# The first super-step of a delta-rule attention and two MoE layers on one core, issued in a new order

## The chip, the core and the metric

The kernel runs on one core of a Trainium2 chip. The core has TensorE (PE: matmuls; its weight loads, PEld, overlap them), VectorE (DVE), ScalarE (ACT), GpSimd (POOL) and SyncE (SP), which issues most of the DMAs. Each engine works through its own queue in order and waits at an instruction until its inputs are there. The metric is the time of one execution on the device in microseconds (us), lower is better.

## The reference

A gated delta rule over 768 positions for 4 x 8 heads of 48 dimensions, and two MoE layers without routing on the 3072 tokens that come out of it:

```python
for t in range(S):
    kt, vt, bt = (k_n[:, :, t], v[:, :, t], beta[:, :, t, None])
    y[:, :, t] = np.einsum('bhd,bhde->bhe', q[:, :, t], state)
    v_old = np.einsum('bhde,bhd->bhe', state, kt)
    state = state + bt[:, :, :, None] * np.einsum('bhd,bhe->bhde', kt, vt - v_old)
...
h = np.maximum(x @ w_in, 0.0); x = h * h @ w_out          # 384 -> 2048 -> 384
g = x @ w_gate; out = g * sigmoid(g) * (x @ w_val) @ w_out2   # 384 -> 1536 -> 384
```

q, k, v and beta are float32; the MoE weights are float64 and reach the chip as pairs of 32-bit words.

## The kernel before

**Super-steps.** The sequence is cut into six super-steps J of 128 positions, each of two chunks c of 64 positions, each with two groups p of heads. For one chunk the recurrence is solved as a block: the gram matrix of k, times -1, a triangular mask and beta, gives M; the inverse of (1 - M) is needed (in NT0 for chunk 0, NT1 for chunk 1); then `ks` (V minus K times state), `u` (inverse times V), `y` (output) and `ku` (new state). Small matmuls in float32 do this on TensorE, with evictions by ScalarE and VectorE.

**The inverse.** For super-step 0 the 16x16 diagonal blocks are inverted on VectorE (`invert16`, once for each chunk). M goes out to DRAM and comes back with one small matrix per partition (`d_out`, `d_in`, tile T), and the result goes home again (`d_home`). Then `dt`, `d1`, `d2` (tiles `ps_dt`, `ps_d`, `ps_e`) merge 16 to 32, and `t11`, `m1`, `m2` (`ps_tq`, `ps_m`, `ps_x`) merge 32 to 64. For later super-steps 32x32 blocks are inverted on GpSimd (`invert`, 60 products and sums, lines 455 and 462), a super-step ahead: `gram`, `mout`, `tload`, `inv`, `nout`, `nback`.

**MoE 1.** For each super-step 16 blocks m of 128 hidden units: `moe1_h` makes `ps_h` (line 784: nine matmuls from x and weight, each split in a high part and a low part: xh, xl, wh, wl), ScalarE and VectorE make `hh` and `hl`, and `moe1_o` adds to `ps_y` (line 810). In super-step 0 the first `HMS[0]` = 14 blocks are done for the first half of the tokens (chunk 0, 256 columns), then again for the second half (chunk 1), so that work can begin before chunk 1 is there; the rest, and the later super-steps but for their first block, run 512 columns wide. MoE 2 comes after all of MoE 1.

**Weights.** 16 pieces (two blocks of `w_in`, or of `w_out`, 768 KB each, the last one in two) are converted from float64: ScalarE takes the absolute value of the upper word (line 173, tile f), VectorE does four integer steps (lines 180, 182, 186, 191, on f and raw), ScalarE writes the high part (line 204), and VectorE or GpSimd subtracts it for the low part (line 207, tile w). `conv(n)` does n of these quarter steps, `need` makes sure of a piece before its use, and during super-step 0 `slot` converts ahead at a rate of CR.

**What sets the order.** TensorE and SP run in the order in which the program is written. In the start (up to `PRE`) VectorE and GpSimd do too, and ScalarE is placed by the scheduler. In the loop that follows only VectorE (and TensorE, SP) keep program order; `timed` spreads the attention's steps over the MoE blocks. V of a chunk is multiplied by the norm (`vn`, line 307); for chunk 1 of super-step 0 this is written behind the inversion of super-step 1, on the same engine. `bank` and the tiles M and ys (two buffers together) limit how far evictions run ahead.

Of the kernel before, what the change touches and what calls it, by code (L numbers as in the profile page):

```python
# [8 lines left out]
F32 = mybir.dt.float32  # L9
# [11 lines left out]
def delta_attention_moe_moe2_kernel(  # L21
# [35 lines left out]
    nc = tc.nc  # L57
# [10 lines left out]
    HMS = [14, 1, 1, 1, 1, 1]  # L68
# [320 lines left out]
    def d_home(c):
        nc.sync.dma_start(  # L390
            out=d_scr[c].rearrange("a g x s t -> (a g x) (s t)"), in_=TF[c * 64:c * 64 + 64, 0:1024]
        )
        for a in range(2):
            for g in range(2):
                p0 = g * 64 + a * 32
                nc.sync.dma_start(
                    out=NT2[c][p0:p0 + 32, :, a * 32:(a + 1) * 32], in_=d_scr[c, a, g].rearrange("x s t -> s x t")
                )
# [68 lines left out]
    def invert16(c):  # L467

        pr = slice(64 * c, 64 * c + 64)
        t_ = TF[pr].rearrange("p (a k) -> p a k", a=2)[:, :, 0:512].rearrange("p a (i j) -> p a i j", j=32)  # L470
        for kk in range(14, 0, -1):
            w = 15 - kk
            tmp = TMP[pr, 0:2 * kk * w].rearrange("p (a i j) -> p a i j", a=2, j=w)
            nc.vector.tensor_tensor(
                tmp,
                t_[:, :, 0:kk, kk:kk + 1].to_broadcast([64, 2, kk, w]),
                t_[:, :, kk:kk + 1, kk + 1:16].to_broadcast([64, 2, kk, w]),
                op=ALU.mult,
            )
            rows = t_[:, :, 0:kk, kk + 1:16]  # L480
            nc.vector.tensor_tensor(rows, rows, tmp, op=ALU.add)
        nc.vector.memset(TF[pr, 0:1024:33], 1.0)

# [195 lines left out]
    def do_y(J, c, p):  # L679
# [3 lines left out]
    STAGES = {  # L683
        "loadk": (k_load, 0), "norm": (k_norm, 0), "nout": (n_out, 0), "gram": (gram, 0.9),
# [5 lines left out]
        "sq": (k_squares, 0), "root": (k_root, 0), "gram0": (gram0, 0.9), "m0": (m0, 0), "dout": (d_out, 0),  # L690
        "din": (d_in, 0), "inv0": (invert16, 0), "dhome": (d_home, 0),
# [236 lines left out]
    order.enter_context(tc.manual_schedule(engines={mybir.EngineType.DVE, mybir.EngineType.Pool}))  # L928

    def conv(n, lo=nc.vector):  # L930
        conv_to(converted() + n, lo)
# [3 lines left out]
    def stage(w, J, c):  # L935
        run_all((w, J, c, p) for p in P2)

    make_identity(nc, ident)
# [6 lines left out]
    nc.gpsimd.memset(AQT[32:64, :, 1], 0.0)  # L945
    for p in P2:
        nc.gpsimd.memset(RSF[p], 0.0)
    nc.sync.dma_start(out=bB, in_=beta)
    run(("loadk", 0, 0))
    run(("loadk", 0, 1))  # L950
    load_w1(0, 0)

    nc.vector.reduce_sum(lower, ident.rearrange("p (b z k) -> p z b k", z=2, k=16)[:, 1], axis=AX.XY)
# [19 lines left out]
    load_w1(1, 0)
    run(("dhome", 1))
    run(("loadk", 1, 1))
    load_w1(1, 1)
    conv(4)
    for w in ("dt", "d1", "d2"):
        run_all((w, 0, p) for p in P2)
    run(("norm", 1, 0))  # L980
    stage("t11", 0, 0)
    stage("m1", 0, 0)
    run(("norm", 1, 1))
    load_w1(2, 0)
    run_all([("gram", 1, 0, 0, True), ("mout", 1, 0, 0)])
    stage("m2", 0, 0)
    run_all([("gram", 1, 1, 0, True), ("mout", 1, 1, 0)])
    conv(3)
    stage("u", 0, 0)
    load_w1(2, 1)  # L990
    stage("y", 0, 0)
    run(("fetch", 0, 0, TOK // 2))
    conv(4)
    run_all([("gram", 1, 0, 1, True), ("mout", 1, 0, 1)])
    stage("ku", 0, 0)
# [3 lines left out]
    for w in ("dt", "d1", "d2"):  # L999
# [8 lines left out]
    conv(4)  # L1008
    PRE = converted()
    startup.clear()  # L1010

# [10 lines left out]
    if True:  # L1022

        LOW2 = 300
        LEAD = 1
        MID = 11
# [3 lines left out]
        CR = 0.75  # L1030
# [17 lines left out]
        timed = spread([L], LEAD, mid) + spread(plan(1, 2, PG, GA, AA, NA, TA), mid, 2 * NM1 + HMS[1] - END)  # L1048
# [127 lines left out]
```

## Time and profile before

| | |
|---|---|
| median of 3 runs | 1242.2 us (1238.1 to 1243.32) |
| profiled execution | 1241.77 us, its span 1239.9 us |
| PE busy | 1099.2 us (89%) |
| PEld, DVE, ACT, POOL busy | 919.8, 626.0, 397.9, 277.9 us |
| mean granted PE clock | 0.944 |

Busy time is the union of an engine's instructions. A timeline row gives start, duration, engine, line, operation, output <- inputs, shapes, count, and in brackets the idle time before it with the instruction that ended that. The granted clock is 1.00 at 2.4 GHz and 0.50 at 1.2 GHz; a mean between them is a mixture.

### The profile page before, as it was taken

What the parts mean: (1) busy time and instruction counts of PE and PEld (TensorE: products, weight loads), DVE (VectorE), ACT (ScalarE), POOL (GpSimd) and SP (SyncE); (2) the same over time, 40 slices, a digit from 0 to 9 for tenths busy, and PEclk for the clock granted to TensorE, in tenths of its full rate; (3) what the DMA queues carried; (4) which work ended last, traced back from release to release, by engine and by line L of the source; (5) the groups of instructions that cost most, each with busy time, mean ns of one, the idle gap of its engine ahead of it and who ended that gap; (6) DMA issues with size and microseconds to landing.
All of it is one profiled execution on the core that took longest, in us unless ns stands there. A gap on an engine that the chain in (4) does not pass through costs nothing. (4 is left out here: it accounts for less than half of the span.)

```text
span 1239.9 us, 25325 instructions
## 1 busy us (share of the span) xinstructions
PE 1099.2 (89%) x10971; PEld 919.8 (74%) x10971; DVE 626.0 (50%) x1034; ACT 397.9 (32%) x753; POOL 277.9 (22%) x396
## 2 busy tenths in 40 slices
PE   3454566799999999999999998799999999999998
PEld 3444555689788888878888876578888888888887
DVE  5751452653664755665545379963434333343333
ACT  1333333334423323332333466631212222121221
POOL 2038321028207405713700023410000000000000
PEclk9977576599999999999999999999999999999999
DMA  7656003443432622613321144510101000010000
GB/s 169 180 116 244 1 7 69 87 108 68 122 80 45 153 66 49 166 44 69 72 56 27 51 154 152 182 48 1 51 1 52 1 31 21 1 51 1 26 1 26
DMA packets 129696, 88.24 MB, mean 71 GB/s; under 512 B 103217, under 2 KB 107953, under 8 KB 129585
## 3 DMA queue, kind: packets, MB, share of 16 engines
q1 hardware_dynamic: 128384, 81.64, 25.4%
q0 software_dynamic: 1056, 4.72, 1.0%
q8 instruction: 86, 1.41, 0.5%
q10 hardware_dynamic: 144, 0.26, 0.1%
q14 instruction: 26, 0.20, 0.1%
HBM read 63.54 MB, written 23.07 MB: 70 GB/s over the span
## 5 line engine op out<-in xcount | busy, mean ns | idle before, releaser
L784 PE MATMUL ps_h<-xh,w 128*128 128x512 f32 (+1 forms) x720 | 222.4, 372 | 46.9 <-DVE w L207 29.0
L784 PEld LDWEIGHTS ps_h<-xh,w 128*128 128x128 f32 x720 | 137.5, 203 | 68.6 <-DVE w L207 29.2
L810 PE MATMUL ps_y<-hh,w 128*128 128x512 f32 (+1 forms) x690 | 165.1, 377 | 10.4 <-ACT w L204 8.7
L877 PE MATMUL ps_g<-x2h,w 128*128 128x512 f32 x432 | 145.7, 392 | 0.5 <-ACT x2h L862 0.5
L787 ACT ACTIVATE r<-ps_h 128x512 f32<-128x512 f32 (+1 forms) x120 | 61.3, 511 | 263.6 <-PE ps_h L784 248.4
L877 PE MATMUL ps_v<-x2h,w 128*128 128x512 f32 x432 | 144.7, 389 | 0.0
L810 PEld LDWEIGHTS ps_y<-hh,w 128*128 128x128 f32 x690 | 119.9, 200 | 30.9 <-ACT w L204 9.1
L881 DVE SCALAR_TENSOR_TENSOR th<-th,ps_g 128x512 f32<-128x512 f32 x72 | 49.5, 687 | 167.6 <-ACT th L880 167.4
L784 PE MATMUL ps_h<-xl,w 128*128 128x512 f32 (+1 forms) x360 | 130.5, 363 | 1.5 <-DVE xl L666 1.5
L794 DVE TENSOR_TENSOR hl<-r,hh 128x512 fp32r<-128x512 f32 (+1 forms) x120 | 79.7, 665 | 88.5 <-ACT r L792 78.8
L790 DVE TENSOR_TENSOR r<-r 128x512 f32<-128x512 f32 (+1 forms) x72 | 49.1, 682 | 135.5 <-ACT hh L788 135.2
L902 PE MATMUL ps_o<-ph,w 128*128 128x512 f32 x432 | 111.9, 389 | 2.7 <-ACT ye L826 2.7
L810 PE MATMUL ps_y<-hl,w 128*128 128x512 f32 (+1 forms) x345 | 89.7, 370 | 13.0 <-DVE hl L794 11.5
L455 POOL TENSOR_TENSOR TMP<-T 128x30 f32<-128x30 f32 (+9 forms) x150 | 82.7, 552 | 79.3 <-DMA T<-m_scr 63.0
L880 ACT ACTIVATE th<-ps_g 128x512 f32<-128x512 f32 x72 | 43.0, 597 | 176.3 <-PE ps_g L877 176.3
L902 PEld LDWEIGHTS ps_o<-ph,w 128*128 128x128 f32 x432 | 81.0, 188 | 19.9 <-ACT ye L826 3.1
L877 PEld LDWEIGHTS ps_g<-x2h,w 128*128 128x128 f32 x432 | 81.7, 189 | 17.9 <-ACT x2h L862 0.9
L207 POOL TENSOR_TENSOR w<-raw,w 128x768 fp32r<-128x768 f32 (+1 forms) x28 | 53.5, 1910 | 184.6 <-ACT w L204 184.6
L877 PEld LDWEIGHTS ps_v<-x2h,w 128*128 128x128 f32 x432 | 81.1, 188 | 16.9
L462 POOL TENSOR_TENSOR T<-T,TMP 128x30 f32<-128x30 f32 (+9 forms) x150 | 87.1, 581 | 11.4
L884 ACT ACTIVATE ph<-th 128x512 fp32r<-128x512 f32 x72 | 45.5, 631 | 133.0 <-DVE th L882 133.0
L877 PE MATMUL ps_g<-x2l,w 128*128 128x512 f32 x216 | 84.8, 392 | 2.7 <-DVE x2l L863 2.7
(116 smaller groups left out, 1853.6 us busy)
## 6 DMA issues: line engine op xcount, KB each, us to landing
raw<-in_moe_w_out_dram SPq DMA_DIRECT2D x13, 768.0 KB, 7.0
raw<-in_moe_w_in_dram SPq DMA_DIRECT2D x8, 768.0 KB, 9.4
KT<-in_kt_dram SPq DMA_DIRECT2D x12, 448.0 KB, 8.1
m_scr<-M SPq DMA_DIRECT2D x20, 256.0 KB, 2.8
KB<-in_kn_dram SPq DMA_DIRECT2D x12, 384.0 KB, 7.1
AQ<-in_q_dram SPq DMA_DIRECT2D x12, 384.0 KB, 7.1
V<-in_v_dram SPq DMA_DIRECT2D x12, 384.0 KB, 4.0
xs_scr<-ys SPq DMA_DIRECT2D x48, 96.0 KB, 2.3
```

The source lines that it names most:

```text
L207: self.lo_eng.tensor_tensor(self.lo, self.v, self.hi.bitcast(F32), op=ALU.subtract)
L455: eng.tensor_tensor(tmp[:, r0:r1], t_[:, r0:r1, kk:kk + 1].to_broadcast([n, r1 - r0, w]), t_[:, kk:kk + 1, kk + 1:].to_broadcast([n, r1 - ...
L462: eng.tensor_tensor(t_[:, r0:r1, kk + 1:], t_[:, r0:r1, kk + 1:], tmp[:, r0:r1], op=ALU.add)
L784: nc.tensor.matmul(ps, w_[:, kk], x_[:, kk, cols], start=n == 0, stop=n == 3 * KD - 1)
L787: nc.scalar.activation(out=r, in_=ps, func=ACTF.Relu)
L790: nc.vector.tensor_tensor(r, r, r, op=ALU.mult)
L794: eng.tensor_tensor(hl[:, at], r, hh[:, at].bitcast(F32), op=ALU.subtract)
L810: nc.tensor.matmul(acc[f], w_[:, fs], h_, start=first, stop=m == NM1 - 1 and n == 2)
L877: nc.tensor.matmul(ps, w_[:, kk], x_[:, kk], start=n == 0, stop=n == 3 * KD - 1)
L881: nc.vector.scalar_tensor_tensor(out=th, in0=th, scalar=1.0, in1=gp, op0=ALU.add, op1=ALU.mult)
L884: nc.scalar.activation(out=hh, in_=th, func=ACTF.Copy)
L902: nc.tensor.matmul(o_acc[J][f], w_[:, fs], h_, start=m == 0 and n == 0, stop=m == NM2 - 1 and n == 2)
```

## The change

The start of super-step 0 is written anew.

- ScalarE is in program order too, up to `PRE`.
- M of super-step 0: `mb0` multiplies mask and beta first (on GpSimd, or VectorE for one group), then `m0` does -gram times that in one operation. It was -gram times mask, then times beta.
- `d_out`, `d_in`, `d_home` become `dmove`: T is loaded right behind M, half of the block DMAs (g = 1) are issued by ScalarE.
- `invert16` treats the two 16x16 blocks of a partition in separate instructions, turn by turn.
- Weight loads, q and later loads come behind the small transfers. `vn` of chunks 0 and 1 is on VectorE, that of chunk 1 no longer behind the inversion. `t11`, `ks`, `m1` of chunk 1 are moved ahead of the MoE.
- `conv(n)` counts whole pieces; three are converted before the loop (before, 17 quarter steps), in gaps of the merge; CR goes from 0.75 to 1.0.
- `HMS[0]` goes from 14 to 8; chunk 1's and super-step 1's steps are spread over fewer blocks (`L` over 0 to 5, `L2` over 5 to 12).

```diff
-    HMS = [14, 1, 1, 1, 1, 1]
+    HMS = [8, 1, 1, 1, 1, 1]
...
-            tmp = TMP[pr, 0:2 * kk * w].rearrange("p (a i j) -> p a i j", a=2, j=w)
...
+            for a in range(2):
+                r0, end = 16 * a, 16 * a + 16
...
+    def d_move(c, out):
...
+                eng = nc.scalar if g else nc.sync
...
-    order.enter_context(tc.manual_schedule(engines={mybir.EngineType.DVE, mybir.EngineType.Pool}))
+    order.enter_context(
+        tc.manual_schedule(engines={mybir.EngineType.DVE, mybir.EngineType.Pool, mybir.EngineType.Activation})
+    )
...
+    run_all(("gram0", 0, p) for p in P2)
+    run(("root", 0, 0))
+    run(("sq", 0, 1))
+    run(("mb0", 0, 0, nc.vector))
+    run(("mb0", 0, 1, nc.gpsimd))
+    run_all(("m0", 0, p) for p in P2)
+    run(("dmove", 0, True))
...
+    run(("inv0", 0))
+    run(("dmove", 0, False))
+    stage("agram", 0, 0)
...
+    run(("inv0", 1))
+    run(("vn", 0, 0, nc.vector))
+    run(("dmove", 1, False))
...
+    merge16("dt", 0)
+    merge16("d1", 0)
+    conv(1)
+    merge16("d2", 0)
...
+    run(("vn", 0, 1, nc.vector))
+    load_w1(3, 0)
+    stage("t11", 0, 1)
...
     run_all(("tload", 1, c) for c in range(2))
     run(("inv", 1, 0, 1, nc.gpsimd))
-    for w in ("dt", "d1", "d2"):
-        run_all((w, 1, p) for p in P2)
-    load_w1(3, 0)
     load_w1(3, 1)
-    run(("v", 0, 1))
-    load_both([4])
-    run(("v", 1, 0))
-    run(("vn", 0, 1))
-    load_both(range(5, NP1))
-    conv(4)
+    conv(1)
     PRE = converted()
+    order.close()
+    order.enter_context(tc.manual_schedule(engines={mybir.EngineType.DVE, mybir.EngineType.Pool}))
     startup.clear()
+    load_both(range(4, NP1))
...
-        CR = 0.75
+        CR = 1.0
...
-        timed = spread([L], LEAD, mid) + spread(plan(1, 2, PG, GA, AA, NA, TA), mid, 2 * NM1 + HMS[1] - END)
+        timed = spread([L], 0, 5) + spread([L2], 5, mid) + spread(plan(1, 2, PG, GA, AA, NA, TA), mid, 2 * NM1 + HMS[1] - END)
```

GpSimd, the end of the inversion of super-step 1 (T, TMP) and what follows it, before; V is chunk 1's values, w a piece's low part:

```order
L455 TENSOR_TENSOR TMP<-T 128x30
L462 TENSOR_TENSOR T<-T,TMP 128x30
L464 MEMSET T 128x32
L307 TENSOR_TENSOR V<-V,nB 128x768
L207 TENSOR_TENSOR w_1489<-raw,w_1489 128x2x384
```

The same engine after, from the middle of that inversion; w_1634, w_1707 and w_1782 are pieces 4 to 6:

```order
L452 TENSOR_TENSOR TMP<-T 128x240
L205 TENSOR_TENSOR w_1634<-raw,w_1634 128x6x128
L459 TENSOR_TENSOR T<-T,TMP 128x16x15
...
L459 TENSOR_TENSOR T<-T,TMP 128x12x19
L205 TENSOR_TENSOR w_1707<-raw,w_1707 128x2x384
...
L205 TENSOR_TENSOR w_1782<-raw,w_1782 128x6x128
...
L461 MEMSET T 128x32
L205 TENSOR_TENSOR w_1857<-raw,w_1857 128x2x384
L667 TENSOR_TENSOR xl<-xr,xh 128x256 x3
```

Low parts that stood behind the whole inversion and the scaling of V now stand between its rows, and that scaling is gone from here.

ScalarE before, from chunk 0's first transpose eviction (td) to its 16x16 merge (NT_103 from ps_e); ps_sq is super-step 1's norm, f and w a weight conversion:

```order
L521 ACTIVATE td<-ps_dt 128x8x16
L332 ACTIVATE ps_sq<-KB 128x384 x2
L521 ACTIVATE td<-ps_dt 128x8x16
L534 ACTIVATE td<-ps_d,lower 128x8x16
L173 ACTIVATE f<-raw 128x768
L534 ACTIVATE td<-ps_d,lower 128x8x16
L547 ACTIVATE NT_103<-ps_e 16x8x16 x4
```

ScalarE after, the same place, with the DMAs that it issues ahead of it (d_scr is the DRAM copy):

```order
L393 DMA NT_103<-d_scr 32x16x32 x2
L393 DMA NT_104<-d_scr 32x16x32 x2
L522 ACTIVATE td<-ps_dt 128x8x16 x2
L535 ACTIVATE td<-ps_d,lower 128x8x16 x2
L171 ACTIVATE f<-raw 128x768 x2
L202 ACTIVATE w_600<-raw 128x6x128
L548 ACTIVATE NT_103<-ps_e 16x8x16 x8
```

The norm is gone from here, two chunks' block DMAs stand ahead, and a whole conversion stands between `td` and the merge.

## Rows read from the trace of the kernel before

**Rows 1.** Stages: us, busy (instructions) of PE, PEld, DVE, ACT, POOL; PEclk; DMA share; GB/s.

```profile
0.00:92.50 92.50, 41.10 (x1472) 38.02 (x1472) 54.89 (x143) 26.41 (x61) 18.45 (x24) 0.91 0.63 154
92.50:137.30 44.80, 14.21 (x209) 13.34 (x196) 11.05 (x16) 11.40 (x28) 35.03 (x62) 0.65 0.46 173
137.30:262.80 125.50, 91.14 (x1092) 82.30 (x1092) 63.02 (x112) 44.88 (x91) 17.95 (x12) 0.64 0.23 50
262.80:306.00 43.20, 43.20 (x767) 39.73 (x766) 18.61 (x35) 18.21 (x44) 29.81 (x51) 1.00 0.35 76
140.00:160.00 20.00, 20.00 (x261) 18.63 (x255) 10.51 (x14) 10.24 (x23) 3.84 (x3) 0.62 0.01 2
```

**Rows 2.** Waits, 93 to 262 us: total us, times, longest.

```profile
PE ps_h L784 <- DVE w L207: 29.0, 1, 29.0
DVE V L598 <- POOL V L307: 27.5, 1, 27.5
```

**Rows 3.** Timeline of GpSimd in two inversions, and one product of VectorE.

```profile
92.21 0.25 POOL L455 TENSOR_TENSOR TMP<-T 128x30 f32<-128x30 f32 x1 [7.49 <-DMA T<-m_scr]
102.30 1.18 POOL L462 TENSOR_TENSOR T<-T,TMP 128x198 f32<-128x198 f32 x1
...
265.62 0.69 DVE L410 TENSOR_TENSOR M<-M,bB 128x512 f32<-128x512 f32 x1
275.24 0.25 POOL L455 TENSOR_TENSOR TMP<-T 128x30 f32<-128x30 f32 x1 [5.18 <-DMA xs_scr<-ys]
276.73 1.47 POOL L307 TENSOR_TENSOR V<-V,nB 128x768 f32<-128x768 f32 x1
285.34 0.64 POOL L462 TENSOR_TENSOR T<-T,TMP 128x198 f32<-128x198 f32 x1
312.18 0.38 POOL L462 TENSOR_TENSOR T<-T,TMP 128x30 f32<-128x30 f32 x1
```

**Rows 4.** Timeline of VectorE, ScalarE and GpSimd, one conversion, 181 to 190 us.

```profile
181.35 0.96 DVE L191 SCALAR_TENSOR_TENSOR raw<-raw 128x768 int32<-128x768 int32 x1
182.41 0.89 ACT L204 ACTIVATE w<-raw 128x768 fp32r<-128x768 f32 x1
183.37 1.85 POOL L207 TENSOR_TENSOR w<-raw,w 128x768 fp32r<-128x768 f32 x1 [6.20 <-ACT w L204]
188.49 0.42 DVE L794 TENSOR_TENSOR hl<-r,hh 128x256 fp32r<-128x256 f32 x1 [6.17 <-ACT r L792]
188.83 0.55 DVE L180 TENSOR_SCALAR f<-f 128x768 f32<-128x768 f32 x1
```

**Rows 5.** Stages, instructions of ps_h only: PE, PEld, ACT; PEclk; DMA; GB/s.

```profile
270.00:280.00 10.00, 2.67 (x18) 2.27 (x18) 0.85 (x3) 1.00 0.65 151
330.00:340.00 10.00, 4.21 (x17) 3.16 (x18) 0.60 (x1) 1.00 0.01 2
```

**Rows 6.** Timeline of TensorE: last blocks of super-steps 0 and 1, first merge of 2.

```profile
306.04 0.28 PE L784 MATMUL ps_h<-xh,w 128*128 128x256 f32 x1
326.69 0.28 PE L573 MATMUL ps_m<-tq,NT 32*32 32x32 f32 x6
407.75 0.28 PE L784 MATMUL ps_h<-xh,w 128*128 128x256 f32 x1
```

**Rows 7.** Timeline of VectorE and ScalarE in the start.

```profile
12.54 1.29 DVE L371 TENSOR_TENSOR NT<-NT,bB 128x512 f32<-128x512 f32 x2
24.63 0.19 DVE L474 TENSOR_TENSOR TMP<-T 64x28 f32<-64x28 f32 x1 [4.57 <-DMA T<-d_scr]
24.86 0.20 DVE L481 TENSOR_TENSOR T<-T,TMP 64x28 f32<-64x28 f32 x1
39.99 0.28 ACT L521 ACTIVATE td<-ps_dt 128x128 f32<-128x128 f32 x1 [24.97 <-PE ps_dt L516]
71.66 0.61 ACT L638 ACTIVATE ys<-ps_y 128x512 f32<-128x512 f32 x1
80.55 1.03 ACT L664 ACTIVATE xh<-xr 128x256 fp32r<-128x256 f32 x3 [4.24 <-DMA xr<-xs_scr]
```

More of the change, by code (lines that the diff above doesn't have):

```diff
@@ L389, in d_home @@
[L389 to L398, printed above, removed]
+        nc.vector.scalar_tensor_tensor(
+            out=NT[c][p], in0=g0.pop((c, p)), scalar=-1.0, in1=NT[c][p], op0=ALU.mult, op1=ALU.mult
+        )
@@ new lines, in d_move @@
+    def d_move(c, out):
+        mats = d_scr[c].rearrange("a g x s t -> (a g x) (s t)"), T[c * 64:c * 64 + 64].rearrange("p a b -> p (a b)")
+        if not out:
+            nc.sync.dma_start(out=mats[0], in_=mats[1])
+        for g in range(2):
+            for a in range(2):
+                p0 = g * 64 + a * 32
+                rows = NT2[c][p0:p0 + 32, :, a * 32:(a + 1) * 32]
+                blocks = d_scr[c, a, g].rearrange("x s t -> s x t")
+                eng = nc.scalar if g else nc.sync
+                if out:
+                    eng.dma_start(out=blocks, in_=rows)
+                else:
+                    eng.dma_start(out=rows, in_=blocks)
+        if out:
+            nc.sync.dma_start(out=mats[1], in_=mats[0])
@@ L469, in invert16 @@
         pr = slice(64 * c, 64 * c + 64)
-        t_ = TF[pr].rearrange("p (a k) -> p a k", a=2)[:, :, 0:512].rearrange("p a (i j) -> p a i j", j=32)
         for kk in range(14, 0, -1):
             w = 15 - kk
-            tmp = TMP[pr, 0:2 * kk * w].rearrange("p (a i j) -> p a i j", a=2, j=w)
[L474 to L482, printed above, removed]
+            steps = []
+            for a in range(2):
+                r0, end = 16 * a, 16 * a + 16
+                tmp = TMP[pr, 64 * a:64 * a + kk * w].rearrange("p (a b) -> p a b", b=w)
+                nc.vector.tensor_tensor(
+                    tmp,
+                    T[pr, r0:r0 + kk, r0 + kk:r0 + kk + 1].to_broadcast([64, kk, w]),
+                    T[pr, r0 + kk:r0 + kk + 1, r0 + kk + 1:end].to_broadcast([64, kk, w]),
+                    op=ALU.mult,
+                )
+                steps.append((T[pr, r0:r0 + kk, r0 + kk + 1:end], tmp))
+            for rows, tmp in steps:
+                nc.vector.tensor_tensor(rows, rows, tmp, op=ALU.add)
+        nc.vector.memset(T[pr].rearrange("p a b -> p (a b)")[:, 0:1024:33], 1.0)
     def n_out(J, pr=slice(0, 128)):
@@ L936, in stage, with merge16 @@
         run_all((w, J, c, p) for p in P2)
-    make_identity(nc, ident)
+    def merge16(w, c):
+        run_all((w, c, p) for p in P2)
+    nc.sync.dma_start(out=bB, in_=beta)
+    run_all(loads(0))
+    nc.gpsimd.memset(AQT[32:64, :, 1], 0.0)
     nc.gpsimd.memset(mask, 0.0)
@@ L944, in delta_attention_moe_moe2_kernel @@
         )
-    nc.gpsimd.memset(AQT[32:64, :, 1], 0.0)
+    make_identity(nc, ident)
+    nc.vector.reduce_sum(lower, ident.rearrange("p (b z k) -> p z b k", z=2, k=16)[:, 1], axis=AX.XY)
+    run(("sq", 0, 0))
+    run_all(("gram0", 0, p) for p in P2)
[5 more added lines that the diff above has]
+    run(("dmove", 0, True))
+    run_all(("gram0", 1, p) for p in P2)
+    load_w1(0, 0)
@@ L946, in delta_attention_moe_moe2_kernel @@
+    run(("loadq", 0))
+    run(("root", 0, 1))
+    run_all(("mb0", 1, p, nc.gpsimd) for p in P2)
+    run_all(("m0", 1, p) for p in P2)
+    run(("dmove", 1, True))
+    run(("v", 0, 0))
+    load_w1(0, 1)
+    run(("inv0", 0))
+    run(("dmove", 0, False))
+    stage("agram", 0, 0)
     for p in P2:
         nc.gpsimd.memset(RSF[p], 0.0)
[L948 to L953, printed above, removed]
@@ L972, in delta_attention_moe_moe2_kernel @@
+    run(("v", 0, 1))
+    load_w1(1, 0)
     run(("loadk", 1, 0))
[L973 to L975 removed]
+    merge16("dt", 0)
+    merge16("d1", 0)
+    conv(1)
+    merge16("d2", 0)
     load_w1(1, 1)
[L977 to L980 removed]
     stage("t11", 0, 0)
     stage("m1", 0, 0)
[L983 removed]
+    run(("loadk", 1, 1))
+    conv(1)
+    stage("m2", 0, 0)
     load_w1(2, 0)
[L985 removed]
@@ L986, in delta_attention_moe_moe2_kernel @@
-    stage("m2", 0, 0)
-    run_all([("gram", 1, 1, 0, True), ("mout", 1, 1, 0)])
-    conv(3)
+    merge16("dt", 1)
     stage("u", 0, 0)
-    load_w1(2, 1)
+    merge16("d1", 1)
     stage("y", 0, 0)
     run(("fetch", 0, 0, TOK // 2))
-    conv(4)
+    run(("norm", 1, 0))
+    merge16("d2", 1)
+    load_w1(2, 1)
+    stage("ku", 0, 0)
+    run_all([("gram", 1, 0, 0, True), ("mout", 1, 0, 0)])
+    run(("norm", 1, 1))
+    run_all([("gram", 1, 1, 0, True), ("mout", 1, 1, 0)])
+    run(("vn", 0, 1, nc.vector))
```

68 lines of the change are left out of this document (21 added, 47 removed).

## The prediction, made before the changed kernel ran

> **What bounds the kernel now.** I read the table of stages first [rows 1]. From 306 us on TensorE is nearly always at work at the full clock, and the program there is the same in both kernels; what the change can win lies before. TensorE is busy 43.2 of 43.2 us from 262.8 to 306, at granted clock 1.00; 91.1 of 125.5 us from 137.3 to 262.8, at 0.64, a mixture of the levels 1.2 and 2.4 GHz; and only 14.2 of 44.8 us from 92.5, where the first MoE matmuls stand, to 137.3. So super-step 0 limps for 170 us.
>
> The waits say why [rows 2]. One wait of TensorE for a converted weight lasts 29.0 us. VectorE should have made that weight, but stood 27.5 us in front of `V <- V - ps_k`, because the scaling of V for chunk 1 is queued on GpSimd behind the 38 us inversion that starts at 92.21 [rows 3]. Later the loss is a loop [rows 4]: VectorE ends a piece's conversion at 182.3, ScalarE writes the high part until 183.3, GpSimd the low part until 185.2; only then can TensorE make the next hidden block, and VectorE's `hl` at 188.49, which needs that block, stands ahead of the next piece's first step at 188.83. A piece costs about 10 us although VectorE works 3.05 us on it (two steps of 0.55, two of 0.96). With 14 blocks in the first half all sixteen full pieces are needed before the second half.
>
> I compare the kernels at one mark: the first hidden matmul of the last block of super-step 0, at 306.04 [rows 6]. Behind it TensorE's order is the same, so time after = 1241.8 - (306.0 - new mark) + what comes late behind the mark. 1241.8 is the profiled execution's own time (span 1239.9); the median of the three runs, 1242.2, differs by 0.03%, so I make no correction.
>
> **The change part by part. (a) The start, up to the first MoE matmul.** T for chunk 0 now loads ahead of the weight and q loads; before, VectorE waited 4.6 us for it and began at 24.63 [rows 7]. M in one operation off the chain saves 0.7 to 1.3 us. I put the first inverse's start at 19.5. But q now stands behind a 768 KB piece, so I give only half of that 5 us to the end of the second inverse. The inverse's 28 steps become 56 halves. The first step of 28 elements starts 0.23 us ahead of the next [rows 7], so 56 cost 12.9 us if each waits for the last, against 7.5 now; two independent 128x512 products took 1.29 us, one alone 0.69 [rows 3, 7], an overlap of 0.09, so that interleaved halves could take 6.5. I take 7, the overlapping row being the same kind of pair; the other end adds 6 us for each of two inverses.
>
> The Trainium skill (VectorE: DVE Perf Modes, section The DRAIN you can't avoid) has the next operation wait until the pipe is empty, and advises fewer operations; by that the halves would cost the 12.9. The overlap of the 128x512 pair speaks against it here; no row shows it for pieces this small.
>
> ScalarE in program order cuts both ways. It issues half of the block DMAs, and those of chunk 1 stand ahead of chunk 0's first transpose eviction `td`: that waits for the second inverse and two transfers, 42 us against 39.99 [rows 7]. A conversion (0.9 + 3.05 + 0.9) now stands ahead of chunk 0's `ps_e` evictions; their matmuls cover perhaps 2 of that. In return two norms and two grams with their evictions, I estimate 6 us, go behind chunk 0. Before, 39.99 to the last `ys` at 72.3 took 32.3 us; I take 32.3 - 6 + 2 = 28, so 70. From `ys` to the fetched x took 8.3 us (72.3 to 80.55) [rows 7]; four gram evictions and chunk 1's transposes and merge, some 8, follow. First MoE matmul: 86, against 92.5; bounds 78 and 98 (both inverses serial).
>
> **(b) The inversion on GpSimd as the new gate.** V's scaling is on VectorE now: the 27.5 us wait goes entirely. Next late is GpSimd. Its inversion of super-step 1 cannot start before the last gram, its multiplies and two transfers, some 10 us after the first MoE matmul: 96 against 92.21. Only pieces 0 to 3 have their low part on VectorE; those of 4, 5 and 6 stand inside the inversion and that of 7 behind it, in GpSimd's order. Block 4 needs piece 4, block 6 needs 6 and 7, so the first half can't end before the inversion does. The undisturbed inversion took 37.3 us, 275.24 to 312.56, with a 1.47 us scaling inside [rows 3]: 36. Four low parts at 1.85 [rows 4] make 7.4, x's low part of the second half some 2.
>
> Conversions on VectorE slow GpSimd. The 128x198 product at 102.30 took 1.18 us beside them, the same shape at 285.34 took 0.64 [rows 3]; that row and the five around it lost some 2.2 us to one piece with its low part, so I estimate 1.6 for a conversion alone. Five pieces fall into the inversion: 8 us. Sum: 36 + 7.4 + 2 + 8 = 53, so the second half starts at 149. Bounds: 46 without the disturbance, 62 if it doubles.
>
> The Trainium skill (SBUF — State Buffer, section Who interferes with whom) says more: the port pair that VectorE shares with GpSimd is an exclusive lock and the loser waits for the whole instruction. By that five conversions would block 15 us, not 8, and the sum would be 7 us more. That row bears out that they disturb each other; it does not show a full block, since VectorE's steps of 0.96 stretched too.
>
> **(c) Eight blocks per half, not fourteen.** A half-width group of nine matmuls takes 1.33 us (2.67 for 18) and a full one 2.23 (4.21 for 17, so 0.248 each) [rows 5]. One full block costs 4.46, two halves 5.34; six blocks save 5.3 us. Conversion has time until block 8, which comes after the second half's eight. A steady super-step takes 407.75 - 306.04 = 101.7 us [rows 6], with two halves and fifteen full blocks; what remains after 149 has eight halves and eight full: 101.7 + 6 x 2.67 - 7 x 4.46 = 86.5, say 87.
>
> To that I add 7 for a low clock: TensorE is sparse until 149, and before, when it came out of such a state, 20 fully busy us from 140 ran at a mean of 0.62 [rows 1]: 0.38 x 20 = 7.6 lost. And 7 for conversions: six of the eight halves each stand beside 3.05 us of conversion and 0.4 of `hl` on VectorE, some 4 us against 2.67 of TensorE. Sum 101; bounds 87 (none of it) and 118 (low clock for all eight halves and what lies beside).
>
> **(d) Behind the mark.** The inversion of super-step 2 starts 9 us after its last M, 266.3 to 275.24 [rows 3], and its block is used at 326.69 [rows 6]: some 64 us after the last gram. In the new order the work between that gram and the same place is five full hidden and output groups, one chunk of attention, the mark, and 20.65 us: some 58. TensorE waits about 5 us there; 0 and 10 are the bounds. Prefetches, resets of RS and moved loads I cost at nothing: they stand beside the inversion or in waits on an engine that is free; a late 768 KB piece would cost some 4 us.
>
> Sum: mark 96 + 53 + 101 = 250, 56 earlier; less 5 gives 51. 1241.8 - 51 = **1190.8; I say 1190**.
>
> **The rivals.** *The gate is early.* If the start gains all that (a) moves and the last gram comes 15 us sooner, GpSimd no longer decides; then conversions do, 8 blocks at 5 to 6 us from 80 on, second half at 128. For it: the start's longest wait in the rows, 4.6 us, is one that the new order of loads removes. Against: four gram evictions in series through two buffers. About 20 us less: 1170.
>
> *The loop stays.* The order is new but the pieces still come just in time, or the start is late by serial halves; the clock stays low for all the second half. About 24 more: 1214. Only the 27.5 us wait would then really be gone. For it: ScalarE and VectorE still work in order, and each high part stands behind the `r` of a block. Against: nothing needs pieces 8 to 16 for eight blocks.
>
> *Slower.* TensorE's clock stays at 1.2 GHz through the whole of super-step 0, the full blocks too, because waits of VectorE between them keep it sparse. [Rows 1] show such a mean (0.64) for 125 us. The remaining 87 us would take 174, some 80 more than my sum has beyond its 7: 1270. It ends on the slower side once over 51 us of the saving is lost, so if more than 58 us of the 87 run low. Against: full blocks with no conversion left kept 1.00 from 262.8 on.
>
> **How the numbers follow.** Forecast 0.58, early gate 0.18, loop stays 0.17, no gain at all (late start and loop together) 0.03, slower 0.04. The range takes in both neighbours and most of the bounds: 1167 to 1217. 0.5%, about what a measurement of this kernel can tell, is 6 us: faster 0.93, same 0.03, slower 0.04.
>
> **What would show it.** (a): the first `ps_h` matmul at 78 to 98, `td` of chunk 0 after the second inverse. (b): no wait of VectorE for V; GpSimd's order with `w` inside T's rows; TensorE waiting for `w` on GpSimd at blocks 4 and 6; the second half at about 149. (c): the mark near 250, clock 1.00 some 20 us before the full blocks. (d): a wait of TensorE before `ps_m` in super-step 2. A mark later than 300, or a new wait of over 20 us behind it, makes the prediction wrong.

## The result, and the profile after

The changed kernel takes 1205.85 us (three runs, 1204.73 to 1207.48); the ratio to the kernel before is 0.972, with a 95% interval of 0.968 to 0.976. So it is 2.8% faster: 36 us, where 51 were forecast. The profiled execution took 1207.48 us, its span is 1205.6, and the three numbers of the prediction's sum can be read in it. TensorE's timeline, first the first MoE matmul, then the first one of the second half, then the mark (the last block of super-step 0):

```profile
95.79 0.58 PE L786 MATMUL ps_h<-xh,w 128*128 128x256 f32 x1
159.16 0.28 PE L786 MATMUL ps_h<-xh,w 128*128 128x256 f32 x1
267.29 0.28 PE L786 MATMUL ps_h<-xh,w 128*128 128x256 f32 x1
```

The mark is 38.75 us earlier than before (306.04, [rows 6]), and behind it 4.45 us are given back: 1205.6 - 267.29 = 938.31 against 1239.9 - 306.04 = 933.86. Together 34.3 us, the difference of the two profiled executions.

The stages in the same columns as [rows 1]:

```profile
0.00:95.80 95.80, 49.67 (x1665) 46.75 (x1665) 49.76 (x192) 27.86 (x71) 17.17 (x23) 0.62 0.55 143
95.80:159.20 63.40, 38.23 (x458) 34.67 (x456) 39.07 (x48) 23.71 (x47) 50.15 (x68) 0.71 0.59 166
159.20:206.00 46.80, 27.89 (x267) 25.05 (x266) 44.83 (x59) 23.06 (x44) 19.16 (x12) 0.80 0.27 69
206.00:267.30 61.30, 59.33 (x1033) 49.00 (x1033) 28.38 (x53) 22.12 (x44) 27.39 (x45) 0.96 0.28 62
```

In the first half GpSimd is busy 50.15 of 63.4 us, in the second half VectorE 44.83 of 46.8, and only from 206 on TensorE: each stage has another bound. What TensorE waits for from 93 to 270 us (total, times, longest):

```profile
PE ps_h L786 <- POOL w L205: 17.8, 2, 9.5
PE ps_m L574 <- issue: 8.9, 1, 8.9
PE ps_y L812 <- DVE hl L796: 8.7, 4, 3.1
```

The 29.0 us for one weight and VectorE's 27.5 us for V [rows 2] are gone. In their place are two waits for low parts that GpSimd makes inside the inversion, one that the profile gives no releaser, and four for `hl`. GpSimd's timeline, the inversion's first and last step, what stands in it and what follows:

```profile
108.01 0.25 POOL L452 TENSOR_TENSOR TMP<-T 128x30 f32<-128x30 f32 x1 [7.88 <-DMA T<-m_scr]
...
128.88 1.84 POOL L205 TENSOR_TENSOR w<-raw,w 128x768 fp32r<-128x768 f32 x1
...
155.64 0.43 POOL L459 TENSOR_TENSOR T<-T,TMP 128x30 f32<-128x30 f32 x1
...
156.09 2.19 POOL L205 TENSOR_TENSOR w<-raw,w 128x768 fp32r<-128x768 f32 x1
158.35 3.62 POOL L667 TENSOR_TENSOR xl<-xr,xh 128x256 fp32r<-128x256 f32 x3
```

It starts at 108.01 (92.21 before, [rows 3]), lasts 48.0 us with three low parts inside (128.88, 137.40, 149.26), and the second half begins as soon as the fourth low part and `xl` are under way.

In the second half VectorE sets the pace. One conversion and the `hl` of two blocks, with GpSimd's low part of the piece before beside them:

```profile
178.88 0.56 DVE L180 TENSOR_SCALAR f<-f 128x768 int32<-128x768 int32 x1
179.48 2.51 DVE L184 SCALAR_TENSOR_TENSOR raw<-raw,f 128x768 int32<-128x768 int32 x1
182.03 0.96 DVE L189 SCALAR_TENSOR_TENSOR raw<-raw 128x768 int32<-128x768 int32 x1
182.90 0.42 DVE L796 TENSOR_TENSOR hl<-r,hh 128x256 fp32r<-128x256 f32 x1
...
187.83 0.42 DVE L796 TENSOR_TENSOR hl<-r,hh 128x256 fp32r<-128x256 f32 x1
```

```profile
179.29 1.88 POOL L205 TENSOR_TENSOR w<-raw,w 128x768 fp32r<-128x768 f32 x1 [3.06 <-ACT w L202]
```

A block takes 4.93 us (182.90 to 187.83) without a gap on VectorE. The step of line 184 takes 0.96 us where no low part stands beside it (at 171.16) and 2.51 here: GpSimd's low part ends at 179.29 + 1.88 = 181.17, and VectorE's step 0.82 us after that. It stands for nearly the whole of the other's instruction.

### The profile page after: what moved, and what is told of

It reads as the page before. It is cut to its first block, busy times and chain, and to the rows that moved or that the text cites. A ratio compares the mean times of both kernels' runs of the same rounds, so it can differ in the third digit from the quotient of the medians.

```text
span 1205.6 us, 25151 instructions
## 1 busy us (share of the span) xinstructions
PE 1088.7 (90%) x10863; PEld 905.6 (75%) x10863; DVE 642.0 (53%) x1080; ACT 393.7 (33%) x735; POOL 293.9 (24%) x400
## 5 line engine op out<-in xcount | busy, mean ns | idle before, releaser
L786 PE MATMUL ps_h<-xh,w 128*128 128x512 f32 (+1 forms) x684 | 215.3, 377 | 21.8 <-POOL w L205 17.8
L812 PE MATMUL ps_y<-hh,w 128*128 128x512 f32 (+1 forms) x654 | 161.1, 383 | 3.3 <-DVE w L205 2.0
L786 PEld LDWEIGHTS ps_h<-xh,w 128*128 128x128 f32 x684 | 129.5, 199 | 44.0 <-POOL w L205 18.3
L812 PEld LDWEIGHTS ps_y<-hh,w 128*128 128x128 f32 x654 | 114.9, 196 | 24.3 <-DVE w L205 2.2
L786 PE MATMUL ps_h<-xl,w 128*128 128x512 f32 (+1 forms) x342 | 125.8, 368 | 1.9 <-POOL xl L667 1.3
L452 POOL TENSOR_TENSOR TMP<-T 128x30 f32<-128x30 f32 (+9 forms) x150 | 86.1, 574 | 79.8 <-DMA NT<-m_scr 38.7
L459 POOL TENSOR_TENSOR T<-T,TMP 128x30 f32<-128x30 f32 (+9 forms) x150 | 90.8, 605 | 11.3
L886 ACT ACTIVATE ph<-th 128x512 fp32r<-128x512 f32 x72 | 45.5, 631 | 133.3 <-DVE th L884 133.3
L812 PEld LDWEIGHTS ps_y<-hl,w 128*128 128x128 f32 x327 | 59.1, 196 | 37.3 <-DVE hl L796 27.7
```

Source lines behind the costliest of these rows:

```text
L452: eng.tensor_tensor(tmp[:, r0:r1], t_[:, r0:r1, kk:kk + 1].to_broadcast([n, r1 - r0, w]), t_[:, kk:kk + 1, kk + 1:].to_broadcast([n, r1 - ...
L459: eng.tensor_tensor(t_[:, r0:r1, kk + 1:], t_[:, r0:r1, kk + 1:], tmp[:, r0:r1], op=ALU.add)
L786: nc.tensor.matmul(ps, w_[:, kk], x_[:, kk, cols], start=n == 0, stop=n == 3 * KD - 1)
L812: nc.tensor.matmul(acc[f], w_[:, fs], h_, start=first, stop=m == NM1 - 1 and n == 2)
L886: nc.scalar.activation(out=hh, in_=th, func=ACTF.Copy)
```

## The experiments

The theory from this profile: **GpSimd's inversion gates the first half, VectorE's conversions pace the second, and a late start costs what is missing.** Rivals: the low clock or the split of blocks costs it; the single wait for V was worth all that was won. Each run has its ratio to runs of the kernel before on the same chip (1243.5 to 1244.9 us; 1242.2 for the changed kernel). Differences between two variants of under some 4 us are within their intervals, and the traces decide there.

| kernel | median us | ratio (95%) |
|---|---|---|
| the changed kernel | 1205.9 | 0.972 (0.968 to 0.976) |
| e1_vn_alone | 1229.0 | 0.988 (0.985 to 0.991) |
| e3_hms14 | 1208.1 | 0.972 (0.969 to 0.975) |
| e5_low_vector | 1202.2 | 0.966 (0.962 to 0.970) |
| e6_cr_half | 1226.9 | 0.987 (0.984 to 0.990) |
| e7_half_rate_2nd | 1198.7 | 0.963 (0.960 to 0.966) |
| e8_ks_late | 1209.7 | 0.971 (0.967 to 0.975) |
| e9_conv_later | 1207.1 | 0.970 (0.966 to 0.974) |
| e10_undivided | 1211.0 | one run |
| e11_bulk_later | 1206.4 | 0.969 (0.966 to 0.972) |
| e12_norm_behind_m1 | 1197.3 | 0.962 (0.958 to 0.965) |
| e13_low_first_half | 1194.5 | 0.958 (0.954 to 0.963) |
| e14_both | 1186.3 | 0.953 (0.950 to 0.956) |

**One part alone, in the kernel before: V on VectorE.**

```diff
-    run(("vn", 0, 1))
+    run(("vn", 0, 1, nc.vector))
```

> The kernel before, with one part of the change alone: the scaling of V of chunk 1 on VectorE instead of GpSimd. Theory A (GpSimd's inversion and then the loop of conversions take over): the 27.5 us wait goes, but pieces still come one in 10 us, and only some 15 us of it reach the end: 1227 us (1220 to 1232). Rival 1 (the wait comes off whole): 1214 us. Rival 2 (the loop swallows it): 1236 or more.

Measured: 1229.0, some 15 us of the 27.5. Behind the wait stands the loop: GpSimd in the inversion, and then pieces just in time (GpSimd's timeline, a low part inside the inversion and its end, then two waits from 93 to 262 us):

```profile
129.55 2.56 POOL L207 TENSOR_TENSOR w<-raw,w 128x768 fp32r<-128x768 f32 x1
...
145.25 0.15 POOL L464 MEMSET T<- 128x32 f32 x1
```

```profile
POOL w L207 <- ACT w L204: 90.4, 7, 44.7
PE ps_h L784 <- ACT w L204: 14.6, 3, 5.3
```

So one moved instruction brings two fifths of the gain, and the rest of the change some 22 us.

**Eight blocks or fourteen.**

```diff
-    HMS = [8, 1, 1, 1, 1, 1]
+    HMS = [14, 1, 1, 1, 1, 1]
```

> The changed kernel with fourteen half-width blocks as before (HMS[0] = 14). Theory A (from the end of GpSimd's inversion VectorE's conversions set the pace, some 4.9 us for each block beside one, and they are the same number in either split): blocks 8 to 13 take 6 x 4.9 = 29 us before the second half, but then only two of its halves carry a conversion; by this 1203 to 1212 us, no difference. Rival 1 (what my prediction had: six blocks less in halves save 5 us of TensorE and the just-in-time loop comes back with 14): 1225 to 1230 us.

Measured: 1208.1, no difference that can be told. TensorE's waits for low parts grow (23.0 us in five instead of 17.8 in two) while the second half gets free of conversions. The split by itself saves nothing, as theory A has it: the conversions, not TensorE, are what either half consists of. My part (c) counted 5.3 us for it.

**Low parts on VectorE.**

```diff
-        N1 = 0
+        N1 = 99
```

> The changed kernel with every low part of super-step 0's weights on VectorE. Theory A (GpSimd's low parts cost twice: 7 to 8 us in its inversion, which gates the first half, and about 1.5 us on VectorE's step beside each, 0.96 against 2.5 us; VectorE's own low part takes 0.95): the second half starts some 8 us sooner and goes 4.4 us a block instead of 4.9: 1194 us (1188 to 1199). Rival 1 (VectorE is the bound by its amount of work, thirteen more instructions of 0.95 add 12 us): 1212 to 1218 us. Rival 2 (neither gates, x of chunk 1 or TensorE's clock does): 1203 to 1208 us.

Measured: 1202.2, some 4 to 7 us less. The second half's pace came as theory A said (4.27 us a block, `hl` at 165.55 and 169.80), but it began only some 3 us sooner (155.98), since the inversion hardly got shorter without a single low part in it:

```profile
107.51 0.25 POOL L452 TENSOR_TENSOR TMP<-T 128x30 f32<-128x30 f32 x1 [7.67 <-DMA T<-m_scr]
...
153.61 0.15 POOL L461 MEMSET T<- 128x32 f32 x1
153.69 3.26 POOL L667 TENSOR_TENSOR xl<-xr,xh 128x256 fp32r<-128x256 f32 x3
```

46.1 us instead of 48.0, although 5.5 us of low parts were taken out. Work moved from GpSimd to VectorE comes back as slower rows on GpSimd. The mark came 10.5 us sooner (256.74), but behind it TensorE waited 5.73 us, until 270.8, for the last low part, which now stood in VectorE's queue; the profiled execution ended 4.4 us sooner.

**Half the rate of conversion.**

```diff
-        CR = 1.0
+        CR = 0.5
```

> The changed kernel with the rate of conversion halved (CR = 0.5), so that four pieces instead of eight stand beside the second half's eight blocks and the rest beside full blocks. Theory A (VectorE's conversions set the second half's pace): its blocks take about 3.4 us on the mean instead of 4.9, 12 us less, and some 4 to 6 us come back in the full blocks, where VectorE has 33 of 61 us free: 1198 us (1192 to 1204). Rival 1 (TensorE's low clock or another engine sets the pace there): 1204 to 1208 us. Rival 2 (pieces late for their blocks again): 1212 us or more.

Measured: 1226.9. Theory A missed by 29 us; rival 2 was right. With fewer pieces ahead, the first half starved: from 95 to 183 us

```profile
PE ps_y L812 <- ACT w L202: 13.0, 3, 7.0
PE ps_h L786 <- ACT w L202: 12.7, 3, 5.7
```

Where little conversion was left beside them, though (one and a half pieces in these 15.7 us), the halves ran as fast as TensorE can:

```profile
183.30:199.00 15.70, 15.70 (x198) 15.12 (x197) 7.22 (x14) 9.61 (x22) 0.00 (x0) 1.00 0.46 114
```

The next run keeps the first half's pieces and takes only the second half's away.

```diff
-                conv_to(PRE + int(STEPS * CR * clock[0]), conv_lo[0])
+                conv_to(PRE + int(STEPS * (min(clock[0], 8) + 0.5 * max(clock[0] - 8, 0))), conv_lo[0])
```

> The changed kernel with conversion at full rate in the first half, so that the pieces of blocks 0 to 7 come as in it, and at half rate from the second half on. Theory A (VectorE sets the pace of the second half): four blocks at 4.9 and four at 2.7 us instead of eight at 4.9, 9 us less up to super-step 1's first ps_m (now 202.75); the four pieces that move into the full blocks find 33 of 61 us of VectorE free and cost 0 to 4: 1200 us (1196 to 1204). Rival (what the half rate lost came from moving conversions at all: they meet super-step 1's attention on VectorE there): 1206 us or more.

Measured: 1198.7, as theory A said. From the second half's start to super-step 1's first `ps_m` took 33.9 us instead of 43.6 (159.18 to 193.09), and 3 us came back in the full blocks (mark 260.73, 6.6 earlier). VectorE was the second half's bound.

**The wait without a releaser.** Before that `ps_m` VectorE's sum over `ps_sq`, behind it `ps_m` itself, in e7 (VectorE's timeline, then TensorE's):

```profile
191.96 1.02 DVE L333 TENSOR_REDUCE NS<-ps_sq 128x8 f32<-128x384 f32 x2
```

```profile
193.09 1.07 PE L574 MATMUL ps_m<-tq,NT 32*32 32x32 f32 x32 [4.84 <-issue]
```

```diff
-        NA = (2, 4)
+        NA = (5, 6)
```

> e7_half_rate_2nd with super-step 2's two norms written behind super-step 1's m1 instead of before it (NA = (5, 6)). In four kernels so far ps_m starts 0.1 us after VectorE's first sum over ps_sq, the profile naming no releaser (202.75 after 202.65 in the changed kernel, 193.09 after 192.98 in e7). Theory C (ps_m waits for the bank that ps_sq holds until then): ps_m starts as soon as its tq is there, 4 us sooner, and the time is 1194 to 1196 us. Rival (the wait is for something else, or another wait takes its place): 1198 us or more.

Measured: `ps_m` at 189.04, right behind the `tq` of 188.52, 4.1 us sooner; the mark came 2.6 us sooner, and the time (1197.3 against 1198.7) is too near to tell. So theory C holds for the wait: `ps_m` wanted the PSUM bank that `ps_sq` held until VectorE had summed it. For the end it was worth little, since a wait for M (2.21 us at 201.62) came in its place.

**The gate's start.**

```diff
-    stage("ks", 0, 1)
-    stage("m1", 0, 1)
...
-        L = chunk(["m2"], 0, 1)
+        L = chunk(["ks", "m1", "m2"], 0, 1)
```

> The changed kernel with ks and m1 of chunk 1 written behind the first MoE block instead of between the grams of super-step 1. Theory A (the inversion's start gates the second half, us for us): the last gram is no longer behind 5.5 us of their matmuls, the inversion starts at 103 to 105 instead of 108.0, and the mark and the time move by the same 3 to 5 us: 1203 us. Rival (chunk 1's chain to its x, or VectorE's conversions, would be late next): chunk 1's ys come some 5 us later and the time stays or grows: 1206 to 1212 us.

Measured: 1209.7; the rival. The inversion started 2.1 us and ended 1.6 us sooner, but the second half was later, first for `xh`, then for `xl` of chunk 1, that now stood behind one more low part on GpSimd:

```profile
160.06 0.58 PE L786 MATMUL ps_h<-xh,w 128*128 128x256 f32 x1 [2.36 <-ACT xh L665]
163.04 0.58 PE L786 MATMUL ps_h<-xl,w 128*128 128x256 f32 x1 [2.40 <-POOL xl L667]
```

The inversion is the last thing before the second half, but chunk 1's own chain is only a few us behind it.

**The start: the conversion in the merge.**

```diff
     merge16("d1", 0)
-    conv(1)
     merge16("d2", 0)
...
     stage("m2", 0, 0)
+    conv(1)
```

> The changed kernel with the first conversion of the merge taken out from between ps_d and ps_e of chunk 0 and put behind chunk 0's m2, where VectorE waits 14.8 us. Theory A (it is on the chain of the start: the ps_e evictions wait for its high part, 47.5 to 51.07): ys of chunk 0 come 2 to 3.5 us sooner, the inversion too, 1204 us (1203 to 1206). Rival (its price is only moved, or the gap is free): 1206 to 1209 us.

Measured: 1207.1; the rival. TensorE reached `ps_e` as early as before, and stopped in the middle of the tile's matmuls with the conversion and without it. In the changed kernel, in e9, and in e3, whose program is the changed kernel's up to there:

```profile
48.75 1.05 PE L543 MATMUL ps_e<-NT,td 32*16 32x16 f32 x99 [2.68 <-issue]
56.22 1.06 PE L556 MATMUL ps_tq<-ident,NT 32*32 32x32 f32 x33 [3.32 <-issue]
62.69 1.01 PE L584 MATMUL ps_x<-NT,tq 32*32 32x32 f32 x31 [2.36 <-issue]
66.28 0.72 PE L517 MATMUL ps_dt<-ident,NT 16*32 16x16 f32 x36 [1.31 <-issue]
```

```profile
51.58 1.03 PE L543 MATMUL ps_e<-NT,td 32*16 32x16 f32 x98 [5.81 <-issue]
59.32 1.06 PE L556 MATMUL ps_tq<-ident,NT 32*32 32x32 f32 x33 [5.36 <-issue]
```

```profile
51.54 1.03 PE L543 MATMUL ps_e<-NT,td 32*16 32x16 f32 x98 [5.81 <-issue]
```

So the longer pause of e9 is not the edit's: e3, with the conversion in its place, has the same. The conversion fits into the pause (ScalarE's evictions of `ps_e` begin at 52.07 in e3 and at 52.11 in e9), and its price was only moved: in e9 it stands ahead of ScalarE's eviction of `ps_x`, and the last `ys` comes at 78.79 (76.66 in e3).

These are not waits for a tile: they come inside one, 127 or 128 matmuls (or twice that) apart, and in all variants of the changed kernel at the same matmuls. The DMA packets in the traces show what ends them. The page of the changed kernel has this queue (packets, MB, share):

```profile
q8 instruction: 85, 1.39, 0.5%
```

That is one packet of 16 KB for every 128 of TensorE's 10863 matmuls. Four of these packets land at 47.46, 54.75, 61.45 and 65.03 us, and TensorE resumes 1.2 to 1.5 us behind each of them (48.75, 56.22, 62.69, 66.28). In every profile each such pause of over 1 us between 40 and 70 us ends 1.2 to 1.7 us behind one (in e3 49.94 and 51.54, in e9 50.04 and 51.58). So TensorE stands there until its next instructions have come. The DMA engines are busy during the first two pauses (share 1.01 from 44 to 60 us), though not during the other two (0.04 from 60 to 70). The next run takes the three weight loads away from there.

```diff
-    load_w1(1, 0)
     run(("loadk", 1, 0))
...
-    load_w1(1, 1)
...
-    load_w1(2, 0)
...
     run(("fetch", 0, 0, TOK // 2))
+    load_both([1])
+    load_w1(2, 0)
```

> The changed kernel with its three 768 KB weight loads that SyncE issues between 44.0 and 48.4 us written behind the fetch of x instead. TensorE stands there in the middle of a tile's matmuls four times (ps_e 2.68, ps_tq 3.32, ps_x 2.36, ps_dt 1.31 us, 9.7 together) and the profile names no releaser; the DMA engines are busy without a gap from 44 to 59. Theory B (TensorE's own instructions are fetched behind these loads): the four waits fall below 4 us together, chunk 0's ys come 4 to 6 us sooner (71 instead of 74.81); what of it is left at the end depends on the later pieces: 1200 to 1207 us. Rival (the waits have nothing to do with the loads): they stay at 8 to 12 us, ys at 74 to 76, and 1206 us or more.

Measured: 1206.4, no difference at the end. The pauses fell from 9.7 to 7.5 us only (`ps_e` 4.45, `ps_tq` 1.50, `ps_dt` 1.51, none in `ps_x`), and to 5.2 in e14 below; the ten profiles with the loads in their old place have 9.7 to 12.9. The first `ys` came at 70.42, 4.4 us sooner, and with it the inversion (103.11) and the second half (155.2). The loads have a part in the pauses, as theory B has it, and the packets show that TensorE's instructions are what is late (in e11 one lands at 49.20, and TensorE resumes at 50.58). Pauses remain where no loads stand beside them, and other transfers (KB, KT) still ran beside `ps_e`. And the 4 us of the start were lost again: `ps_m` came at 201.75, 1 us sooner. VectorE was busy for 42.9 of the 46.6 us before it, as in the changed kernel; that its pace is what lost them was argued, not shown.

**The inverse undivided.**

```diff
-            for a in range(2):
-                r0, end = 16 * a, 16 * a + 16
...
+            tmp = TMP[pr, 0:2 * kk * w].rearrange("p (a i j) -> p a i j", a=2, j=w)
```

> The changed kernel with the 16x16 inverses undivided again, 28 steps instead of 56 halves. If interleaved halves overlap (6.5 us for 56 in the changed kernel's trace), the 28 steps take 7 to 7.5 us and chunk 0's td comes 1 to 2 us later. If instead each step paid for itself, 28 would take about half of 56: 3.3 us.

VectorE's timeline, first step and the end of chunk 0's inverse, undivided, then in the changed kernel:

```profile
19.44 0.19 DVE L471 TENSOR_TENSOR TMP<-T 64x28 f32<-64x28 f32 x1 [1.34 <-DMA T<-d_scr]
...
26.91 0.09 DVE L479 MEMSET T<- 64x32 f32 x1
```

```profile
19.35 0.25 DVE L473 TENSOR_TENSOR TMP<-T 64x14 f32<-64x14 f32 x2 [1.23 <-DMA T<-d_scr]
...
25.87 0.09 DVE L483 MEMSET T<- 64x32 f32 x1
```

28 steps 7.47 us, 56 halves 6.52: the halves gain 1 us, they do not cost 5. `td` did not move with it (43.41 against 43.59), so that the 1 us is hidden there.

**Versions that beat both.** e12 with the low parts of the first half on VectorE, and that with the later loads:

```diff
-        N1 = 0
+        N1 = 8
```

> e12_norm_behind_m1 with the low parts of the pieces begun in the first half on VectorE. By e5_low_vector, where GpSimd's inversion without any low part inside still took 46 us and the second half began 2.5 us sooner: 2 to 3 us less than e12. Rival (VectorE's seven more instructions cost what the inversion gains): the same as e12 or 2 us more.

> e13_low_first_half with the later weight loads of e11_bulk_later. In e11 the second half began 4 us sooner (155.2 against 159.2), but super-step 1's first ps_m only 1 us sooner (201.75 against 202.75), and nothing reached the end. Theory A (VectorE's eight conversions set the second half's pace there, so that an earlier start of it is lost): with four of them moved away, as in e13, the earlier start comes through: 1190 to 1192 us against 1194.5. Rival (the later loads cost elsewhere what the start gains): 1194 to 1197 us.

Measured: 1194.5 (1187.1 to 1196.9), the 2 to 3 us that were expected (the intervals overlap), and 1186.3 (1181.8 to 1192.2), more than expected, though the two ranges overlap: 19 to 20 us under the changed kernel, 4.7% under the one before. The way to it was not theory A's. The inversion started 6.4 us sooner in e14 (102.56 against 108.94), but the second half at the same place (156.91 against 156.88), since VectorE's low parts gated it. What differs is the clock. From the second half's start (in e14 from 0.4 us behind it) to `ps_m`, and from there to the mark, first e13, then e14:

```profile
156.88:182.16 25.28, 22.81 (x223) 20.88 (x223) 21.08 (x32) 14.85 (x29) 7.86 (x7) 0.83 0.51 126
182.16:254.15 71.99, 65.87 (x1072) 54.32 (x1073) 42.29 (x82) 28.29 (x57) 32.86 (x49) 0.91 0.23 53
```

```profile
157.30:178.34 21.04, 19.97 (x222) 18.91 (x221) 19.62 (x31) 15.12 (x29) 1.97 (x1) 0.96 0.46 107
178.34:245.67 67.33, 61.52 (x1073) 50.46 (x1074) 43.95 (x82) 28.18 (x57) 32.59 (x48) 0.97 0.26 57
```

Together 97.3 us in e13 and 88.8 in e14, with the 0.4, for the same matmuls, with a granted clock of 0.83 and 0.91 in the one and 0.96 and 0.97 in the other (means of the levels 1.2 and 2.4 GHz). In e13 the second half began with three waits for `xl` (1.30, 0.39 and 0.39 us); in e14 `xl` was there. Whether these waits kept the clock down was not tested, nor whether the clock would be the same in another execution: that of the start was not (below).

## Why the prediction was right, and where its sum was off

The forecast (1190, range 1167 to 1217) holds the time, and the mechanisms came in the order that it named: the wait for V gone, GpSimd's inversion next late, waits for low parts at blocks 4 and 6, TensorE short of work until the second half, a wait before super-step 2's `ps_m`. But its sum was 16.7 us short against the profiled execution, and little in it cancelled: (a) and (c) are short by 19 us, (b) and (d) give back 2.4. That the range holds the time is owed to its width, which was drawn to take in the neighbour at 1214. The steps:

| step | forecast | measured | difference |
|---|---|---|---|
| (a) inversion starts | 96 | 108.01 | +12.0 |
| (b) to the second half | 53 | 51.15 | -1.85 |
| (c) to the mark | 101 | 108.13 | +7.1 |
| (d) given back behind it | 5 | 4.45 | -0.55 |

**(a) is the step that failed.** Its first half was near: inverse from 19.35, 6.5 us for each, `td` at 43.59 (42 said). Then ScalarE's timeline, the last `ys`, and the fetched x:

```profile
76.52 0.60 ACT L639 ACTIVATE ys<-ps_y 128x512 f32<-128x512 f32 x1 [1.11 <-PE ps_y L633]
...
83.28 1.03 ACT L665 ACTIVATE xh<-xr 128x256 fp32r<-128x256 f32 x3 [2.37 <-DMA xr<-xs_scr]
```

`ys` ended at 77.1 instead of 70: I let 6 us of norms and grams go, and 9.7 us of pauses on TensorE, which have nothing to do with the order of ScalarE, stayed (the kernel before has 9.0 of them between 41 and 60 us). Without the three loads there, in e11, this piece took the 28 us that I had given it (43.57 to 72.5: 28.9), and 27.6 in e14. The low clock is not the cause. It was 0.50 nearly all the way in the changed kernel's profile and 1.00 in e10's, and neither the matmuls nor the whole took less there. The changed kernel, then e10, `td` to `ys`:

```profile
43.59:77.12 33.53, 21.43 (x918) 19.97 (x921) 9.15 (x13) 14.46 (x36) 0.00 (x0) 0.50 0.52 147
43.41:77.55 34.14, 21.43 (x918) 19.96 (x921) 9.16 (x13) 14.47 (x36) 0.00 (x0) 1.00 0.55 145
```

Then x took 2 us less than said, and the work up to the first MoE matmul 12.5 instead of 8. The change puts `ks` and `m1` of chunk 1 ahead of the MoE, and my 8 us had no term for `ks`: TensorE works 3.6 us at `ps_k` there, and 1.9 at `ps_m`. With both behind the first block, in e8, the rest took 6.6. The changed kernel, then e8:

```profile
83.30:95.80 12.50, 10.27 (x241) 9.85 (x233) 11.27 (x21) 6.62 (x17) 7.74 (x6) 0.55 0.37 103
82.57:89.15 6.58, 4.31 (x142) 3.87 (x137) 5.67 (x12) 4.55 (x12) 3.63 (x3) 0.92 0.43 138
```

The clock has little part in that: e3 took 11.8 us at 0.66. The inversion then started 12.2 us behind the first MoE matmul, not 10. The conversion in the merge, that I charged with 2 us, cost nothing that could be shown (e9).

**(b) was right, and so were its terms.** 48.0 us with 5.5 of low parts inside leave 6.5 above the undisturbed 36; I had 8 for five conversions, and four whole ones fell into it, so 1.6 us for each, as said. The Trainium skill (SBUF — State Buffer, section Who interferes with whom) has the loser of the shared ports wait for the whole instruction, and by that the sum would have been 7 us more. The trace agrees for one direction only: VectorE's step stood for nearly all of GpSimd's low part (2.51 us), while the inversion's rows stretched to 1.13 to 1.40 us and the whole came out below my 8. In the rows that I had read of before the two never met like this: there VectorE's step was over when the low part began [rows 4].

**(c) had the right work and the wrong pace.** Up to `ps_m` the eight halves took 43.6 us; my sum had 8 x 2.67 + 7 + 7 = 35.4 for them. I took 4 us for a block beside a conversion; it is 4.93, because GpSimd's low part blocks VectorE (e5: 4.27 without it). Six blocks had a whole conversion beside them, as said, and the first of these, with `xl` and two low parts on GpSimd, took 7.5 us (`hl` at 160.43 and 167.97). The bank held by `ps_sq` is in it too. The clock's 7 us were not to be added on top: TensorE was waiting there anyway (busy for 27.9 of the 46.8 us from 159.2). Nor was the clock at 1.00 for 20 us before the full blocks, as my sign had it: it was 0.80 in that stretch. The other eight blocks took 64.5 us, 65.6 said. And the reason that I gave for eight blocks, 5.3 us of TensorE, is not seen (e3).

**(d) was right in size**: 4.45 us. But of TensorE's waits around super-step 2's `ps_m` only 0.85 and 0.22 us are the forecast one, for the inverse. 2.76 us came before them, for an `hl` that stood on VectorE behind a norm, and the norm had waited 2.25 and 1.51 us for GpSimd's squares, which my sum did not have.

**The rivals.** The early gate (1170) did not come, since the start was late. The time lies nearer to the loop that stays (1214) than to my 1190, but not by its mechanism: the halves of the inverse were not serial (e10), and the clock did not stay low for all the second half (0.80 from 159 to 206, 0.96 from there to the mark). What it had right is that VectorE's conversions still set a pace, for 44 us instead of 125. The slower case needed a low clock through the full blocks, too.

## To carry to other kernels

When a wait is taken away, ask at once for the next two that stand behind it, and test the part alone: here 15 of 27.5 us were the wait's own, and the rest had to be won from GpSimd, VectorE and the loads one after the other. Two engines that hold each other up are one resource: count their work together. Four conversions moved in time, into blocks where both have room, gave 7 us (e7); low parts moved from the one to the other gave 4 to 7 of the 12 that were expected (e5). A gain ahead of a stage that another engine gates need not arrive: 4 us were lost in e11, and in e14 the inversion came 6.4 us sooner and the second half no sooner. And when work is put ahead of a mark, give it a term: `ks`, moved ahead of the MoE, had none.

## What the runs showed of the hardware

- VectorE and GpSimd: a step of 0.96 us beside a low part of 1.88 us took 2.51 us. An inversion with three low parts inside took 48.0 us, one with none inside 46.1 (e5), 48.1 (e13) or 45.5 (e14).
- TensorE pauses of 1.3 to 5.8 us inside one tile's small matmuls, without a releaser, the longest while the DMA engines are full; it resumes 1.2 to 1.7 us behind a packet of 16 KB of the queue for instructions. The same program had 2.68 us at `ps_e` in one execution and 5.81 in another (the changed kernel's and e3's); with three loads fewer beside them the sum was 7.5 and 5.2 us instead of 9.7 to 12.9.
- The granted clock of the same start differs between executions: 0.50 from 20 to 70 us in the changed kernel's profile, 1.00 in e8's, which has the same program there; and 1.00 in the kernel before, 0.50 in e1. The 918 small matmuls from `td` to `ys` were busy for 21.43 us at either level.
- The granted clock did not touch the 32x32 transposes: 1.06 us for such a group at 0.50 (1.2 GHz; the row at 56.22 above) and at 1.00 (2.4 GHz), in the kernel before:

```profile
53.55 1.06 PE L555 MATMUL ps_tq<-ident,NT 32*32 32x32 f32 x32 [1.51 <-issue]
```

The grams follow it: in the changed kernel one half of a gram's matmuls from 86.7 to 88.75 us, at 0.50, and from 209.5 to 210.7, at 1.00 (busy us, mean ns):

```profile
L358 PE MATMUL ps_g<-KT 48*64 48x64 f32 x16 | 2.0, 314 | 0.0
...
L358 PE MATMUL ps_g<-KT 48*64 48x64 f32 x16 | 1.1, 221 | 0.0
```
